# Linear attention, then a top-2 mixture of experts: the order in which the engines' instructions are emitted in the experts with seven products

## The chip, the cores and the metric

One core of one Trainium2 chip runs the kernel. Its time is the device time of one execution in microseconds; what is compared is the median of several runs of each kernel.

## The reference

Shapes: batch 4, 8 heads, 768 positions, 64 channels a head; so 3072 tokens of 512 channels. There are 8 experts with w1 of 512 x 1024 and w2 of 1024 x 512, all in fp32.

```python
# attention with a decay lam[h], in blocks of 64 positions
for b in range(nb):
    intra = einsum('bhic,bhjc->bhij', qb, kb) * Dmask
    intra = einsum('bhij,bhjd->bhid', intra, vb)
    inter = einsum('bhid,bhde->bhie', qb * lam_pow, kv_state)
    out[:, :, sl] = intra + inter
    kv_state = lam_block * kv_state + einsum('bhsd,bhse->bhde', kb * rev_pow, vb)
# mixture: every token goes to its two best experts
noisy = x @ w_gate + log1p(exp(x @ w_noise)) * noise
top2_w = softmax of the two largest of noisy
for e in range(E):
    h = maximum(x[mask] @ w1[e], 0.0)
    out[mask] += top2_w[mask, k, None] * (h @ w2[e])
```

## The kernel before

A first part computes the attention, the gate and the lists of tokens of each expert. Expert 0 and expert 1 then run with plain matrix products. Experts 2 to 7, ordered by how many tokens they have, are what the change is about. Each takes 768 or 800 tokens: six tiles of 128 and, for experts 2 to 4, one tile of 32. Every fp32 operand is split into a high part, which an activation rounds to fp32r, and a low part, the difference, which a subtraction makes; a product is three matmuls (high x high, high x low, low x high).

*First layer.* An expert's 2 x 2 block product (tokens and channels halved) is done with seven block products instead of eight, for each of four pairs of column blocks, f = 0 to 3. Function `first_layer` walks a list of 26 slots, `SEQ`: five for f=0, then seven for each of f = 1, 2, 3, in which products 4 and 3 of f-1 stand between products 2 and 6 of f. Products 4 and 3 of f=3 come later (`ENDS`), after the first 18 matmuls of the second layer. A product is six matmuls (L969) of 384 or 400 columns into a PSUM bank: U, V (four banks named pS) or W (pR or pL). Products 1, 6 and 7 all accumulate in U, and after each ScalarE copies U to SBUF (L992, a tile "ot"); PE's next product into U waits for that copy. The "ot" tiles come from a pool of four buffers, which the stores of turned rows and, in experts 2 to 4, the crossed tiles use as well.

`result` makes the hidden values out of the banks: an add on DVE (L981: bank plus copy), ScalarE's activation for the high part (L975), and the low part, on DVE (L978) or, for products 2 and 7, a further activation (L986) and a subtraction on POOL (L987). All of it stands at the product's own slot. At fixed slots stand besides: the splits of w2 (`split_w`: L829 on ACT, L833 on DVE) and of the column blocks f = 2, 3 of w1 (`split_c`, three groups: L804 on ACT, L805 on DVE; after group 1 four sums of weight blocks on POOL, L808 to L811, which group 2 then splits), the loads of later weights, and for the next expert the gathers of its rows on POOL (L876), each behind a one-element copy "spacer" (L1383), and their turning on DVE (L896) and storing by SP (L898). `gather_prev` (L1038) reads the earlier output.

*Second layer.* `gemm2` multiplies tile by tile into two banks, pO and pKV, by turns; DVE evacuates each (L1080 or L1082) and POOL scatters it to the output (L1126). Experts 2 to 4 do three of the tiles as columns (`columns2`), four steps ahead of the four row tiles. Between tiles `behind` prepares the next expert: `operands` (its split and combined rows: L937 on ACT, L938 and L943 to L946 on DVE) and `split_c` of the blocks f = 0, 1.

The whole program is emitted in a fixed order: every engine does its instructions in the order in which the code emits them. A tile from a pool waits until the instructions that used the buffer before are done.

Of the kernel before, what the change touches and what calls it, by code (L numbers as in the profile page):

```python
# [37 lines left out]
E = 8  # L38
# [85 lines left out]
def kernel(  # L124
# [666 lines left out]
    def split_c(e, f, group):  # L791
# [12 lines left out]
        nc.scalar.activation(hi[:, ks], src, AF.Copy)  # L804
        nc.vector.tensor_tensor(lo[:, ks], src, hi[:, ks].bitcast(FT), op=SUB)  # L805
        if group == 1:
            g = nc.gpsimd
            g.tensor_tensor(a22, a21, a22, op=ADD)  # L808
            g.tensor_tensor(a21, a11, a21, op=SUB)  # L809
            g.tensor_tensor(a11, a22, a11, op=SUB)  # L810
            g.tensor_tensor(a12, a12, a11, op=SUB)  # L811
# [160 lines left out]
    def result(e, f, m, banks):  # L972

        def high(i, k, src):
            nc.scalar.activation(hv(e, 0, i, k), src, AF.Relu)  # L975

        def low(i, k, src, eng):
            eng.scalar_tensor_tensor(hv(e, 1, i, k), src, 0.0, hv(e, 0, i, k).bitcast(FT), op0=OP.max, op1=SUB)  # L978

        def add(i, k, p, x, eng):  # L980
            nc.vector.tensor_tensor(x, p, x, op=ADD)  # L981
            high(i, k, x)
            if eng is nc.vector:
                low(i, k, x, eng)
            else:
                nc.scalar.activation(x, x, AF.Relu)  # L986
                eng.tensor_tensor(hv(e, 1, i, k), x, hv(e, 0, i, k).bitcast(FT), op=SUB)  # L987

        U, V, W = [banks.get(b) for b in "UVW"]
# [12 lines left out]

    LOWS = (nc.gpsimd, nc.gpsimd, nc.vector)
# [359 lines left out]
    def first_layer(e):  # L1363

        banks = {f: {} for f in range(QF)}
        nxt = tile_order(e + 1) if e + 1 < E else []
        for s, (f, m) in enumerate(SEQ):
            product(e, f, m, banks[f])
            result(e, f, m, banks[f])
            pace = banks[f][1][0:1, 0:1]  # L1370
            if s in (0, 2, 12, 17):
                j = (0, 2, 12, 17).index(s)
                split_w(2, e, j)
                if j < 2:
                    load_j(e, j + 2)
            for g, at in enumerate(((5, 12), (8, 15), (9, 16))):
                if s in at:
                    split_c(e, 2 + at.index(s), g)
            if s in (11, 18) and e + 1 < E:
                load_c(e + 1, (11, 18).index(s))  # L1380
            for i, j in enumerate(nxt):
                if s == (0, 1, 4, 7, 9, 14, 16)[i]:
                    nc.gpsimd.tensor_copy(spacer, pace)  # L1383
                    gather_rows(e + 1, j)
                if s == (6, 8, 13, 15, 20, 22, 22)[i]:
                    turn_rows(e + 1, j)
            if s in (2, 5, 10, 12):
                gather_prev(e, (0, 1, 3, 4)[(2, 5, 10, 12).index(s)])
        return banks[QF - 1]

    def behind(e, t, steps):

        if e + 1 == E:
            return
        n = e + 1
# [148 lines left out]
```

## Time and profile before

| | |
|---|---|
| median of 3 runs | 852.26 us (850.43 to 856.97) |
| profiled execution | 848.9 us, its span 847.1 |
| granted clock of TensorE, mean | 0.944 |
| busy: PE, DVE, ACT, POOL | 720.6, 438.8, 337.7, 394.7 us |
| six first layers | 287.8 us |

A busy time is an engine's sum over the span; the matmuls are pipelined, so PE's is no measure of full speed. Where an engine waited, the profile names the instruction whose semaphore came last.

### The profile page before, as it was taken

What the parts mean: (1) busy time and instruction counts of PE and PEld (TensorE: products, weight loads), DVE (VectorE), ACT (ScalarE), POOL (GpSimd) and SP (SyncE); (2) the same over time, 40 slices, a digit from 0 to 9 for tenths busy, and PEclk for the clock granted to TensorE, in tenths of its full rate; (3) what the DMA queues carried; (4) which work ended last, traced back from release to release, by engine and by line L of the source; (5) the groups of instructions that cost most, each with busy time, mean ns of one, the idle gap of its engine ahead of it and who ended that gap; (6) DMA issues with size and microseconds to landing.
All of it is one profiled execution on the core that took longest, in us unless ns stands there. A gap on an engine that the chain in (4) does not pass through costs nothing.

```text
span 847.1 us, 14367 instructions
## 1 busy us (share of the span) xinstructions
PE 720.6 (85%) x4861; PEld 627.0 (74%) x4861; DVE 438.8 (52%) x1009; ACT 337.7 (40%) x670; POOL 394.7 (47%) x569
## 2 busy tenths in 40 slices
PE   6999998999999696887869877987687977798696
PEld 4888887889898585776759666876575766587584
DVE  6348796842655754455454645373435444453421
ACT  2667855112432244423542345324442354235400
POOL 6022657786354557324832385226722573244322
PEclk9999999999999889999999988998998999989998
DMA  9999975652546655337533663347533453343001
GB/s 203 216 252 258 254 210 178 222 121 50 174 126 174 158 136 151 111 85 185 189 110 99 184 175 118 107 127 191 154 108 98 122 183 100 101 119 99 10 37 33
DMA packets 165728, 121.29 MB, mean 143 GB/s; under 512 B 89597, under 2 KB 136829, under 8 KB 165652
## 3 DMA queue, kind: packets, MB, share of 16 engines
q1 hardware_dynamic: 151076, 84.04, 36.7%
q0 software_dynamic: 14160, 35.77, 16.4%
q8 instruction: 39, 0.64, 0.3%
q10 hardware_dynamic: 416, 0.53, 0.2%
q14 instruction: 37, 0.30, 0.1%
HBM read 83.87 MB, written 37.32 MB: 143 GB/s over the span
## 4 chain that ended last, share of the span: by engine, by line
PE 33%; issue 16%; DVE 15%; POOL 14%; ACT 9%; SPq 8%; DMA 5%; POOLq 0%; DVEq 0%; ACTq 0%
PE pS L1016 8%; PE pKV L1064 6%; PE pO L1064 4%; SPq L910 4%; POOL out_dram L1126 3%; ACT ht L975 3%; ACT w L804 3%; DVE ot L981 2%; DVE w L805 2%; PE pS L364 2%; PE pKV L377 2%; SPq L781 2%; PE pS L969 2%; PE pO L377 2%; POOL wst L809 2%
## 5 line engine op out<-in xcount | busy, mean ns | idle before, releaser
L969 PE MATMUL pS<-xa,w 128*128 128x400 f32 (+1 forms) x624 | 183.4, 375 | 82.6 <-ACT ot L992 80.4
L969 PEld LDWEIGHTS pS<-xa,w 128*128 128x128 f32 x624 | 124.2, 205 | 102.5 <-ACT ot L992 96.1
L1064 PE MATMUL pO<-w2h,ht 128*128 128x512 f32 x336 | 113.0, 407 | 13.2 <-DVE pv L1080 6.8
L1064 PE MATMUL pKV<-w2h,ht 128*128 128x512 f32 x336 | 112.9, 407 | 11.5 <-DVE w1b L1080 11.5
L805 DVE TENSOR_TENSOR w<-wst,w 128x512 fp32r<-128x512 f32 (+2 forms) x72 | 56.1, 792 | 116.1 <-ACT w L804 116.1
L987 POOL TENSOR_TENSOR ht<-ot,ht 128x400 fp32r<-128x400 f32 (+1 forms) x48 | 49.3, 1027 | 98.0 <-ACT ot L986 86.6
L804 ACT ACTIVATE w<-wst 128x512 fp32r<-128x512 f32 (+2 forms) x72 | 48.7, 692 | 106.2 <-POOL wst L811 57.9
L969 PE MATMUL pS<-xb,w 128*128 128x400 f32 (+1 forms) x240 | 88.9, 370 | 0.0
L1064 PEld LDWEIGHTS pO<-w2h,ht 128*128 128x128 f32 x336 | 65.9, 196 | 29.4 <-DVE pv L1080 8.1
L1064 PEld LDWEIGHTS pKV<-w2h,ht 128*128 128x128 f32 x336 | 65.8, 196 | 27.3 <-DVE w1b L1080 12.4
L975 ACT ACTIVATE ht<-ot 128x400 fp32r<-128x400 f32 (+1 forms) x72 | 38.2, 531 | 91.3 <-DVE ot L981 91.3
L1016 PE MATMUL pS<-xa,w 128*128 128x256 f32 (+2 forms) x440 | 73.5, 316 | 0.8 <-DVE xa L888 0.4
L1016 PEld LDWEIGHTS pS<-xa,w 128*128 128x128 f32 x440 | 65.3, 189 | 4.8 <-DVE xa L888 0.6
L1064 PE MATMUL pO<-w2l,ht 128*128 128x512 f32 x168 | 68.1, 405 | 0.0
L1064 PE MATMUL pKV<-w2l,ht 128*128 128x512 f32 x168 | 68.0, 405 | 0.0
L833 DVE TENSOR_TENSOR w2l<-wst,w2h 128x1024 fp32r<-128x1024 f32 (+1 forms) x33 | 38.4, 1163 | 44.7 <-ACT w2h L829 44.5
L876 POOL DMA_INDIRECT xr<-x_tok,rec x42 | 48.7, 1161 | 17.1 <-issue 7.5
L631 POOL DMA_INDIRECT lst<-recs,dest x48 | 48.4, 1009 | 11.0 <-issue 8.1
L969 PEld LDWEIGHTS pS<-xb,w 128*128 128x128 f32 x240 | 50.4, 210 | 0.5
L808 POOL TENSOR_TENSOR wst<-wst 128x256 f32<-128x256 f32 x24 | 18.1, 756 | 64.8 <-DVE w L805 55.7
L992 ACT ACTIVATE ot<-pS 128x400 f32<-128x400 f32 (+1 forms) x72 | 34.9, 485 | 30.0 <-PE pS L969 19.3
L937 ACT ACTIVATE xa<-wst 128x512 fp32r<-128x512 f32 (+1 forms) x48 | 24.8, 565 | 53.5 <-DVE wst L946 53.5
(300 smaller groups left out, 1458.7 us busy)
## 6 DMA issues: line engine op xcount, KB each, us to landing
wst<-in_moe_w_dram SPq DMA_DIRECT2D x36, 512.0 KB, 4.5
turned<-ot SPq DMA_DIRECT2D x36, 256.0 KB, 3.5
kt<-in_k_dram SPq DMA_DIRECT2D x24, 256.0 KB, 5.7
qt<-in_q_dram SPq DMA_DIRECT2D x24, 256.0 KB, 6.0
vt<-in_v_dram SPq DMA_DIRECT2D x24, 256.0 KB, 5.7
wst<-in_moe_w_dram SPq DMA_DIRECT2D x48, 128.0 KB, 2.6
wst<-in_moe_w_dram SPq DMA_DIRECT2D x96, 64.0 KB, 2.8
wst<-turned SPq DMA_DIRECT2D x96, 64.0 KB, 2.0
```

Of the source, the lines that this page charges most:

```text
L377: nc.tensor.matmul(PO[u][a][half(g), hp, :], lhs, rhs, start=n == 1, stop=n == (8 if u % NW or a else 4))
L631: st = nc.gpsimd.indirect_dma_start(out=lst, out_offset=bass.IndirectOffsetOnAxis(ap=r["dest"][:, i, c:c + 1], axis=0), in_=r["rec"][:, c, ...
L804: nc.scalar.activation(hi[:, ks], src, AF.Copy)
L805: nc.vector.tensor_tensor(lo[:, ks], src, hi[:, ks].bitcast(FT), op=SUB)
L833: low.tensor_tensor(lo, st, hi.bitcast(FT), op=SUB)
L876: nc.gpsimd.indirect_dma_start(out=xrow(e, t)[:size(e, t)], out_offset=None, in_=x_tok[:rows, :], in_offset=bass.IndirectOffsetOnAxis(ap=a ...
L969: nc.tensor.matmul(p, WO[f % 2][:, a, kw, d, :], xo(x, kx, kx + 1)[:, 0, d, :w], start=first and i == 0, stop=i == 5, skip_group_check=True)
L975: nc.scalar.activation(hv(e, 0, i, k), src, AF.Relu)
L987: eng.tensor_tensor(hv(e, 1, i, k), x, hv(e, 0, i, k).bitcast(FT), op=SUB)
L992: nc.scalar.activation(banks[m], U, AF.Copy)
L1016: nc.tensor.matmul(p, W1[a][d][:, fs], xt(b, cs)[:, d], start=(d == 0 and i == 0), stop=(d == DB - 1 and i == 2))
L1064: nc.tensor.matmul(p, h, W2[b][f // 2][:, f % 2, :], start=(i == 0), stop=(i == len(TERMS) - 1))
```

## The change

`result` no longer emits its instructions but returns lists of them: those for the product's own slot, the next slot and the one after that. Product 7 begins with the next slot and makes its low part on DVE now, from the sum and without the further activation. `first_layer` keeps a table `todo` of what stands at each slot; the lists of `result` are appended to it, after what the table held from the start. The splits, sums, loads, gathers and turnings get slots of their own, the sums of POOL four slots ahead of group 2, the high and low halves of a split mostly a slot apart. The spacer copies in front of the gathers are gone. `behind` is called before a tile instead of after it, and splits groups 0 and 1 (with the sums) a tile ahead of group 2.

```diff
-    def split_c(e, f, group):
+    def split_c(e, f, group, what="hl"):
...
-        nc.scalar.activation(hi[:, ks], src, AF.Copy)
-        nc.vector.tensor_tensor(lo[:, ks], src, hi[:, ks].bitcast(FT), op=SUB)
-        if group == 1:
-            g = nc.gpsimd
-            g.tensor_tensor(a22, a21, a22, op=ADD)
...
+        if "h" in what:
+            nc.scalar.activation(hi[:, ks], src, AF.Copy)
+        if "l" in what:
+            nc.vector.tensor_tensor(lo[:, ks], src, hi[:, ks].bitcast(FT), op=SUB)
+
+    def sums_c(e, f):
...
+        g = nc.gpsimd
+        g.tensor_tensor(a22, a21, a22, op=ADD)
...
     def result(e, f, m, banks):
...
         if m == 2:
-            add(f, 0, W, banks[1], LOWS[0])
-        elif m == 7:
-            add(f + QF, 1, V, banks[7], LOWS[1])
-        elif m == 4:
-            high(f + QF, 0, U)
-            low(f + QF, 0, U, nc.vector)
-        elif m == 3:
-            add(f, 1, V, banks[6], LOWS[2])
-
-    LOWS = (nc.gpsimd, nc.gpsimd, nc.vector)
+            x = banks[1]
+            return [[add(W, x)], [high(f, 0, x), positive(x)], [rest(f, 0, x)]]
+        if m == 7:
+            x = banks[7]
+            return [[], [add(V, x)], [high(f + QF, 1, x)], [low(f + QF, 1, x)]]
+        if m == 4:
+            return [[high(f + QF, 0, U)], [low(f + QF, 0, U)]]
+        if m == 3:
+            x = banks[6]
+            return [[add(V, x)], [high(f, 1, x)], [low(f, 1, x)]]
+        return []
...
     def first_layer(e):
...
+        for j, s in enumerate((1, 6, 13, 20)):
+            at(s, lambda j=j: split_high(2, e, j))
+            at(s + 1, lambda j=j: split_low(2, e, j))
+            if j < 2:
+                at(s + 1, lambda j=j: load_j(e, j + 2))
+        for c, ss in ((2, (3, 8, 12)), (3, (10, 15, 19))):
+            for g, s in enumerate(ss):
+                at(s, lambda c=c, g=g: split_c(e, c, g, "h"))
+                at(s + (g != 1), lambda c=c, g=g: split_c(e, c, g, "l"))
+            at(ss[1], lambda c=c: sums_c(e, c))
+            if e + 1 < E:
+                at(ss[2] + 1, lambda c=c: load_c(e + 1, c - 2))
+        for i, j in enumerate(nxt):
+            at((0, 1, 4, 7, 9, 14, 16)[i], lambda j=j: gather_rows(e + 1, j))
+            at((6, 8, 13, 15, 20, 22, 22)[i], lambda j=j: turn_rows(e + 1, j))
+        for i, j in enumerate((0, 1, 3, 4)):
+            at((2, 5, 10, 12)[i], lambda j=j: gather_prev(e, j))
+
+        def step(s, f, m):
+            product(e, f, m, banks[f])
+            ops = result(e, f, m, banks[f])
+            if ops and s < len(SEQ):
+                for op in ops[0]:
+                    op()
+            for op in todo.pop(s, []):
+                op()
+            if ops and s >= len(SEQ):
+                for op in ops[0]:
+                    op()
+            for i, more in enumerate(ops[1:]):
+                at(s + 1 + i, *more)
...
-            if s in (0, 2, 12, 17):
-                j = (0, 2, 12, 17).index(s)
-                split_w(2, e, j)
-                if j < 2:
-                    load_j(e, j + 2)
-            for g, at in enumerate(((5, 12), (8, 15), (9, 16))):
-                if s in at:
-                    split_c(e, 2 + at.index(s), g)
-            if s in (11, 18) and e + 1 < E:
-                load_c(e + 1, (11, 18).index(s))
-            for i, j in enumerate(nxt):
-                if s == (0, 1, 4, 7, 9, 14, 16)[i]:
-                    nc.gpsimd.tensor_copy(spacer, pace)
-                    gather_rows(e + 1, j)
...
+    def behind(e, t):
...
+        c, x = {1: ((1, 3), (2, 3, 4, 5))}.get(e, ((0, 3), (2, 4, 5, 6)) if e in CROSS else ((0, 2), (1, 3, 4, 5)))
+        for i, k in enumerate(c):
+            if t == k:
+                split_c(n, i, 0)
+                split_c(n, i, 1)
+                sums_c(n, i)
+            if t == k + 1:
+                split_c(n, i, 2)
+                load_c(n, i + 2)
         for p in range(4 if TAILS[n] else 3):
-            if t == at[p]:
+            if t == x[p]:
                 operands(n, p)
...
+            behind(e, t)
+            last(tile)
...
-            behind(e, t, len(steps))
```

## Rows read from the trace of the kernel before

**Rows 1.** Waits of PE, whole span: us in total, times, longest us.

```profile
PE pS L969 <- ACT ot L992: 80.4, 44, 5.1
PE pKV L1064 <- DVE w1b L1080: 11.5, 2, 5.8
PE pO L1064 <- DVE pv L1080: 6.8, 3, 2.4
PE pO L1064 <- DVE w1b L1082: 6.4, 1, 6.4
```

**Rows 2.** Windows: first layers of experts 2 to 7; us and instructions by engine.

```profile
core 0: us, PE busy (x) PEld busy (x) DVE busy (x) ACT busy (x) POOL busy (x), PEclk, DMA share, GB/s
304.84:352.73 47.89, 35.05 (x159) 31.82 (x158) 24.27 (x38) 23.21 (x42) 30.24 (x34) 0.89 0.48 141
393.19:442.85 49.66, 34.62 (x158) 30.83 (x159) 24.14 (x42) 24.30 (x46) 32.24 (x40) 0.93 0.50 144
483.94:533.88 49.94, 35.92 (x159) 32.97 (x158) 23.43 (x37) 24.25 (x45) 32.08 (x38) 0.86 0.49 139
576.48:626.39 49.91, 34.56 (x158) 31.07 (x157) 22.05 (x33) 23.55 (x44) 31.56 (x38) 0.90 0.50 138
670.16:715.66 45.50, 32.62 (x158) 30.09 (x157) 21.89 (x33) 22.09 (x41) 28.18 (x34) 0.92 0.50 141
759.22:804.11 44.89, 33.23 (x158) 29.88 (x157) 18.11 (x27) 21.98 (x41) 19.85 (x22) 0.92 0.23 57
```

**Rows 3.** Timeline of PE in expert 5: start, us, instruction.

```profile
594.38 0.33 PE L969 MATMUL pS<-xb,w 128*128 128x384 f32 x1
...
595.42 0.34 PE L969 MATMUL pS<-xb,w 128*128 128x384 f32 x1
```

**Rows 4.** Windows in expert 5, behind a long wait and later; columns as in rows 2.

```profile
585.20:592.00 6.80, 5.78 (x18) 5.78 (x19) 2.16 (x3) 4.28 (x8) 4.57 (x7) 0.50 0.69 206
597.50:612.00 14.50, 8.42 (x42) 7.15 (x42) 6.27 (x11) 7.01 (x14) 9.86 (x12) 1.00 0.50 150
```

**Rows 5.** Waits of ACT from 300 us on; columns as in rows 1.

```profile
ACT ht L975 <- DVE ot L981: 91.3, 72, 5.0
```

**Rows 6.** Timeline of ACT in expert 5, idle time before in brackets.

```profile
611.55 0.47 ACT L992 ACTIVATE ot<-pS 128x384 f32<-128x384 f32 x1
615.54 1.06 ACT L804 ACTIVATE w<-wst 128x1024 fp32r<-128x1024 f32 x1 [3.52 <-POOL wst L811]
```

**Rows 7.** Timeline of PE at the same place.

```profile
612.08 0.44 PE L969 MATMUL pS<-xa,w 128*128 128x384 f32 x1 [4.69 <-ACT ot L992]
```

**Rows 8.** POOL's instructions by line from 304 us: min/median/max ns, first and last start.

```profile
L987 POOL TENSOR_TENSOR ht<-ot,ht x48: 989/1022/1066, 310.8 to 806.5; 128x400 fp32r<-128x400 f32 x24, 128x384 fp32r<-128x384 f32 x24
L808 POOL TENSOR_TENSOR wst<-wst x22: 720/732/767, 322.4 to 790.1; 128x256 f32<-128x256 f32 x22
L876 POOL DMA_INDIRECT xr<-x_tok,rec x32: 951/1060/2146, 309.0 to 700.0; - x32
```

**Rows 9.** Timeline of POOL: last scatter of the expert before, experts 2 to 6.

```profile
307.14 1.44 POOL L1126 DMA_INDIRECT out_dram<-w1b,rec  x1 [3.13 <-DVE ovi L1334]
...
399.14 1.36 POOL L1126 DMA_INDIRECT out_dram<-ot,rec  x1 [0.27 <-issue]
...
489.15 1.36 POOL L1126 DMA_INDIRECT out_dram<-ot,rec  x1 [0.26 <-issue]
...
582.64 1.35 POOL L1126 DMA_INDIRECT out_dram<-ot,rec  x1 [0.27 <-issue]
...
671.39 1.58 POOL L1126 DMA_INDIRECT out_dram<-ot,rec  x1 [0.51 <-DVE ot L1082]
```

**Rows 10.** Timeline of DVE in the second layer of expert 5.

```profile
638.81 0.68 DVE L938 TENSOR_TENSOR xb<-wst,xa 128x512 fp32r<-128x512 f32 x1
...
642.24 1.29 DVE L938 TENSOR_TENSOR xb<-wst,xa 128x512 fp32r<-128x512 f32 x2 [0.70 <-ACT xa L937]
...
648.80 1.22 DVE L805 TENSOR_TENSOR w<-wst,w 128x1024 fp32r<-128x1024 f32 x1 [4.33 <-ACT w L804]
```

**Rows 11.** DMA issues of the page: KB each, median us from issue to landing.

```profile
turned<-ot SPq DMA_DIRECT2D x36, 256.0 KB, 3.5
```

More of the change, by code (lines that the diff above doesn't have):

```diff
@@ L803, in split_c @@
             ks = slice(0, 2)
[L804 to L811 removed]
+        if "h" in what:
[3 more added lines that the diff above has]
+    def sums_c(e, f):
+        v = WS[1, e, f].rearrange("p (d i c) -> p d i c", d=DB, i=2)
+        a11, a12, a21, a22 = [v[:, 2 * j:2 * j + 2, i, :] for i in range(2) for j in range(2)]
+        g = nc.gpsimd
+        g.tensor_tensor(a22, a21, a22, op=ADD)
+        g.tensor_tensor(a21, a11, a21, op=SUB)
+        g.tensor_tensor(a11, a22, a11, op=SUB)
+        g.tensor_tensor(a12, a12, a11, op=SUB)
     def split_w(which, e, j, half=None, low=nc.vector):
@@ L972, in result, with low, positive, rest @@
     def result(e, f, m, banks):
+        U, V, W = [banks.get(b) for b in "UVW"]
         def high(i, k, src):
[L975 to L989, printed above, removed]
+            return lambda: nc.scalar.activation(hv(e, 0, i, k), src, AF.Relu)
+        def low(i, k, src):
+            return lambda: nc.vector.scalar_tensor_tensor(hv(e, 1, i, k), src, 0.0, hv(e, 0, i, k).bitcast(FT),
+                                                          op0=OP.max, op1=SUB)
+        def positive(x):
+            return lambda: nc.scalar.activation(x, x, AF.Relu)
+        def rest(i, k, x):
+            return lambda: nc.gpsimd.tensor_tensor(hv(e, 1, i, k), x, hv(e, 0, i, k).bitcast(FT), op=SUB)
+        def add(p, x):
+            return lambda: nc.vector.tensor_tensor(x, p, x, op=ADD)
         if m in (1, 6, 7):
@@ L1389, in first_layer, with at @@
-        return banks[QF - 1]
-    def behind(e, t, steps):
-        if e + 1 == E:
-            return
-        n = e + 1
-        at = (1, 4, 5, 6) if e in CROSS else (0, 1, 3, 4) if e > 1 else (1, 2, 4, 5)
+        todo = {}
+        def at(s, *ops):
+            todo.setdefault(s, []).extend(ops)
+        for j, s in enumerate((1, 6, 13, 20)):
[3 more added lines that the diff above has]
+                at(s + 1, lambda j=j: load_j(e, j + 2))
@@ L1401, in behind @@
                     load_j(n, p)
-        for c, k in enumerate((0, 2) if e in CROSS else (0, 2)):
-            if t == k:
-                for g in range(3):
-                    split_c(n, c, g)
-                load_c(n, c + 2)
     def fetch_pairs(e):
@@ L1438 @@
         else:
-            bank = first_layer(e)
+            step, todo = first_layer(e)
         if e == E - 1:
@@ L1452 @@
             next(steps[0])
-            for f, m in ENDS:
-                product(e, f, m, bank)
-                result(e, f, m, bank)
+            for i, (f, m) in enumerate(ENDS):
+                step(len(SEQ) + i, f, m)
+            for s in sorted(todo):
+                for op in todo[s]:
+                    op()
             next(steps[1])
@@ L1462 @@
             prepare(e + 2)
-        for t, step in enumerate(steps):
+        for t, tile in enumerate(steps):
             if e == 1:
                 turn_next(t + FB - LAG)
-            last(step)
+            behind(e, t)
+            last(tile)
             if e in CROSS:
```

11 lines of the change are left out of this document (4 added, 7 removed).

## The prediction

> **What bounds the kernel now.** The waits of PE come first [rows 1]: one kind makes up most of its idle time after the attention, 80.4 us in 44 waits, at most 5.1 us each, of the product line L969 on the ScalarE copy L992. All lie in six stretches, the first layers of experts 2 to 7, which take 47.89, 49.66, 49.94, 49.91, 45.50 and 44.89 us, together 287.8 [rows 2]. The same rows show that no engine is full there: PE is busy 33 to 36 us of each, POOL 20 to 32, DVE 18 to 24, ACT 22 to 24, and the granted clock is 0.86 to 0.93. How little PE needs shows in its timeline: the second matmul of one half product starts at 594.38 and that of the half product after the next at 595.42, so a product at full clock is 1.04 us [rows 3], and by the ratio of the columns 1.08 where it has 400 instead of 384 (experts 2 to 4). Twenty-six products are 27.0 or 28.2 us; three layers of each, 166 us. So 287.8 - 166 = 122 us are idle time or half clock. The clock is the second half of the price of a stall: behind the 5.1 us wait it was granted at 0.50, the 1.2 GHz level, for the whole stretch 585.2 to 592.0, and at 1.00, 2.4 GHz, in 597.5 to 612.0 [rows 4].
>
> Why PE waits is read from ACT: 91.3 us in 72 waits (one for each such activation) of L975 on the add L981 on DVE [rows 5]. ACT takes its instructions in order, so whatever stands behind an add that is not there yet waits too, and L992 is one of them. An example: the copy for slot 16 of expert 5 (product 6 of f=2) is done only at 612.02 [rows 6], and product 7 starts at 612.08 after 4.69 us idle [rows 7]. A second such point is group 2 of a weight split: ACT idles 3.52 us to 615.54 for POOL's last sum, with copies queued behind [rows 6].
>
> **The change, part by part.** (1) *Results over three slots.* The add stays at its slot (for product 7 it moves one slot on), the activation and the subtraction follow one and two slots later. No matmul is added or taken. The copies L992, which PE needs soonest, are still emitted first in their slot, now behind activations whose add was emitted a slot earlier. DVE gets four more subtractions per expert, and POOL loses four of 1.02 us [rows 8]; ACT loses four activations (the positive part for product 7). None of the three was full, so I cost it at nothing: DVE's 18 to 24 us become 20 to 26 beside PE's 27 to 28, and if PE went below that DVE would be the bound. (2) *The spacer copies of POOL go*, and with them the wait of a gather for a copy and of an add for a spacer. The gathers are then paced by POOL's queue alone. (3) *Sums ahead of group 2:* groups 0, 1 and 2 of a column split move from slots 5, 8, 9 and 12, 15, 16 to 3, 8, 12 and 10, 15, 19. The four sums of POOL, 0.73 us each with 0.08 between, 3.3 us in all [rows 8], now have four slots, 4.2 us, before ACT asks for them. The loads of the next two column blocks go from slots 11 and 18 to 13 and 20, those of W2 from 0 and 2 to 2 and 7, and W2's splits from 0, 2, 12, 17 to 1, 6, 13, 20 with the subtraction a slot later. SP issues the loads in order with the stores of the turned rows, and those of slots 13 and 20 now stand right ahead of a store. I cost that below, with the buffers.
>
> What is late next? I follow POOL's queue, since its sums feed group 2, and group 2 feeds products 6, 5, 7 and 3 (slots 16 and 23). POOL is free of the last expert's scatters at 308.58, 400.50, 490.51, 583.99 and 672.97 [rows 9], which is 3.7, 7.3, 6.6, 7.5 and 2.8 us after the starts of experts 2 to 6 [rows 2]. Ahead of the first sums stand four gathers and two reads of earlier output, all indirect transfers, for which I take the gather's 1.06 us [rows 8] and 0.25 of issue as between the scatters [rows 9]: 6 x 1.31 = 7.9; one subtraction 1.0; the sums 3.3. So the sums end 12.2 us after POOL is free. From there: ACT's part of group 2 takes 1.06 us [rows 6] and DVE's 1.22 [rows 10], and slot 16 starts at +2.3. POOL meanwhile does a subtraction, four indirect transfers and the second sums, 1.0 + 5.2 + 3.3 = 9.5, and slot 23 starts 2.3 later, at +11.8, where PE alone would have come at +2.3 + 7 x 1.05 = +9.7. Three products more give +15. One more us I add because the copy of slot 12 may take the buffer that POOL's subtraction of slot 8 gives back: it stands right behind the sums in POOL's queue. So a layer ends 12.2 + 16 = 28.2 us after POOL is free: 31.9, 35.5, 34.8, 35.7 and 31.0 us. Expert 7 has no gathers, so PE sets its time: 27.0 and some 2 of waits, 29.0. Together 197.9 against 287.8: 89.9 us less.
>
> To that I add a reserve of 4.5 us a layer, 27 us. One part is the clock: the 6.8 us at 0.50 in [rows 4] lost half their work, 3.4 us, and I keep half of such a loss, 1.7. The other, 2.8 us, is for waits that such a reckoning leaves out, above all for the four "ot" buffers. A value now holds its buffer two slots longer, and a store of turned rows takes 3.5 us from issue to landing [rows 11]. At the low end this is nothing; at the high end two copies of a layer wait one store each on the path, 7 us, in the five layers with turned rows. I take 2.8, nearer to the low end because two of the four buffers come free by DVE and not by a store. First layers: 89.9 - 27 = 63 us less.
>
> (4) *The second layers* (`behind`). Their waits are evacuations that DVE reaches late: 11.5 us in two for experts 5 and 6, 6.8 in three for experts 2 to 4, 6.4 for expert 1 [rows 1]. In expert 5 DVE idles 4.33 us for group 2, then does 1.22 of it, and only then the evacuation [rows 10]. Now group 2 comes a tile later. For experts 5 and 6 group 2 and the operands still stand ahead of the second tile's evacuation, and the operands alone are 4.7 us of DVE, from 638.81 to 643.53 [rows 10]. The sums start earlier, though, before the first tile's evacuation: the second tile is out some 3 us sooner, and of 5.8 us idle about 3 remain; I take 3 us less each, between 5 less and 1 more. For expert 1 the split group and the operands no longer meet ahead of one evacuation: 5 less, between 8 and 0. For experts 2 to 4 the change puts 4.7 us of operands *ahead* of the first row tile's evacuation, which PE already awaits. That adds up to 4.7 at the place; PE gets some back since fewer operands are left at the end: 2 more each, between 0 and 5. Sum: -5 - 6 + 6 = -5, between -18 and +17.
>
> In all 848.9 - 63 - 5 = 781 us for the profiled execution; it lies 3.4 us under the median of the three runs, 852.26, so on that scale 784.
>
> A rule that speaks against part (1): VectorE now works more beside POOL's sums. In the rows a sum took 0.720 to 0.767 us in all 22 cases, whatever DVE did [rows 8]. The Trainium skill (GPSIMD Engine Reference, 8. Key points) says that GpSimd shares its SBUF interfaces with VectorE, with contention when a DVE instruction has two SBUF inputs. By that the two sums of a layer would lengthen and every layer with them; the trace shows no such spread, so the reckoning stands without it.
>
> **The rivals.** *Buffers bind* (784 + 35 = 819): the high end of the buffer term, two stores of 3.5 us [rows 11] on the path in each of five layers. For it: four buffers, and at slots 20 to 23 all are held, while the stores stand in SP's queue behind six weight loads. Against: the allocator has so far found buffers such that only short waits came of it.
>
> *Nothing but POOL's list binds* (784 - 27 - 8 = 749): the reserve is not needed and the second layers reach the better half of their bounds. For it: after the change no engine waits in order for a chain of its own making. Against: all engines stay coupled.
>
> *The wait stays* (852): ACT's queue is still in order, and group 2 in slots 12 and 19 still stands ahead of copies. If each of the ten indirect transfers ahead of the second sums took twice its 1.31 us, slot 23 would come 13 us later, in five layers 66 us, all of the gain; the change would then do only on paper what it says. Against: POOL idles now; its 32 us of work in a stretch of 50 [rows 2] shrink by over 4.
>
> *Slower, by the clock* (about 874): the few long idle stretches become many short ones, and PE is granted 1.2 GHz nearly throughout. A product then takes 2.08 us, a layer 54 or 56, six of them 331; with a tenth of the work at 2.4 GHz 315, 27 us more than now, of which part (4) gives back 5. It decides from the point where the mean clock of the first layers falls under 166/288 = 0.58. Against it: 597.5 to 612.0 holds several short idle stretches (8.42 us busy of 14.50) at a clock of 1.00 [rows 4]. The Trainium skill (TensorE: Matmul & The Clock Gate, A second HAM failure mode) tells of a kernel whose PE idled briefly between groups of matmuls and whose clock swung between the levels; the stretch named speaks against that here.
>
> **How the numbers follow.** Forecast 784, chance 0.60; buffers bind 0.17; POOL alone 0.13; the wait stays 0.06; slower 0.04. The forecast's own range, with the bounds of part (4), is 771 to 806. To leave out no more than 2 in 10 the whole must reach to 822 for the buffers and into the POOL case, to 755. A measurement tells about 1% from nothing: faster by more than that 0.90, within it 0.06, slower 0.04.
>
> **What would show it.** Right: the six first layers last 30 to 40 us each, the waits of L969 on L992 fall under 30 us, the granted clock there rises to 0.95; L975 no longer waits 91 us for L981; the wait of ACT for POOL's last sum shrinks but does not vanish in experts 3 to 5, being shortest in expert 7. The second layers of experts 2 to 4 get longer, those of 1, 5 and 6 shorter. Wrong, if ACT's copies wait for stores or for POOL in the buffers' name, if POOL's gathers wait for turned rows ahead of the sums, or if DVE, with most of the moved work, becomes the engine that the copies' readers wait for.

## The result, and the profile after

The changed kernel takes 813.3 us (median of 3 runs, 811.66 to 816.01) beside 852.26: ratio 0.9536, 95% interval 0.9463 to 0.961. That is 39 us less, where 68 were forecast; it lies near the rival *Buffers bind* (819). The profiled run has a span of 811.5 us.

In the code after the change the product is L975 (was L969), ScalarE's copy out of bank U L1000 (L992), the activation L983 (L975), the add L996 (L981), GpSimd's subtraction L993 (L987), the weight splits L805 and L807 (L804, L805), the sums L814 to L817 (L808 to L811), the evacuation L1089 (L1080).

Windows of the first layers of experts 2 to 7, columns as in [rows 2]:

```profile
306.70:353.32 46.62, 32.79 (x158) 31.27 (x157) 26.04 (x41) 21.08 (x39) 25.52 (x26) 0.90 0.56 157
397.00:445.78 48.78, 34.78 (x158) 33.35 (x157) 25.80 (x37) 20.36 (x38) 26.71 (x28) 0.83 0.52 153
489.33:533.14 43.81, 34.07 (x159) 32.71 (x158) 24.82 (x36) 20.40 (x38) 25.93 (x27) 0.84 0.50 147
577.35:621.48 44.13, 32.07 (x158) 30.29 (x157) 24.68 (x36) 20.02 (x38) 25.60 (x27) 0.88 0.50 145
659.38:700.63 41.25, 31.12 (x158) 30.17 (x157) 24.06 (x36) 20.02 (x38) 25.20 (x25) 0.92 0.54 148
738.57:768.17 29.60, 28.58 (x158) 27.19 (x157) 21.65 (x30) 20.53 (x38) 19.63 (x19) 1.00 0.35 87
```

Together 254.2 us, 33.6 less than before. Expert 7, which turns no rows for a next expert, came down to 29.6; the other five lost only 1 to 6 us each, and their granted clock is 0.83 to 0.92 still.

The waits of PE that answer to [rows 1], and below them those of ScalarE from 300 us on that answer to [rows 5]:

```profile
PE pS L975 <- ACT ot L1000: 59.6, 19, 5.7
PE pO L1073 <- DVE pv L1089: 13.6, 3, 4.6
PE pKV L1073 <- DVE w1b L1089: 4.9, 4, 1.4
```

```profile
ACT ot L1000 <- POOL ht L993: 45.3, 10, 5.6
...
ACT ot L1000 <- DMA turned<-ot: 23.8, 6, 6.1
...
ACT w L805 <- POOL wst L817: 14.5, 5, 4.1
ACT ot L1000 <- DMA out_dram<-ot,rec: 12.3, 8, 2.4
ACT ot L1000 <- DVE ht L986: 8.6, 6, 1.8
ACT ht L983 <- DVE ot L996: 5.3, 8, 0.8
```

The wait for the add fell from 91.3 us in 72 to 5.3 in 8, as the change means it to. In its place the copies wait before they start, for a buffer to write into: 45.3 us in ten waits, two in each of five layers, for GpSimd's subtraction, and 23.8 for stores of turned rows. PE's waits became fewer (19 for 44) and longer.

One such place, in expert 5: the timelines of ScalarE, of GpSimd and of PE.

```profile
593.08 0.49 ACT L1000 ACTIVATE ot<-pS 128x384 f32<-128x384 f32 x1 [2.51 <-DMA turned<-ot]
...
598.63 0.87 ACT L1000 ACTIVATE ot<-pS 128x384 f32<-128x384 f32 x2 [4.13 <-POOL ht L993]
...
608.91 0.49 ACT L1000 ACTIVATE ot<-pS 128x384 f32<-128x384 f32 x1 [5.44 <-POOL ht L993]
```

```profile
604.79 0.72 POOL L814 TENSOR_TENSOR wst<-wst 128x256 f32<-128x256 f32 x1 [0.48 <-DVE w L807]
605.59 0.72 POOL L815 TENSOR_TENSOR wst<-wst 128x256 f32<-128x256 f32 x1
606.39 0.72 POOL L816 TENSOR_TENSOR wst<-wst 128x256 f32<-128x256 f32 x1
607.20 0.72 POOL L817 TENSOR_TENSOR wst<-wst 128x256 f32<-128x256 f32 x1
607.88 0.99 POOL L993 TENSOR_TENSOR ht<-ot,ht 128x384 fp32r<-128x384 f32 x1
```

```profile
609.45 0.69 PE L975 MATMUL pS<-xa,w 128*128 128x384 f32 x1 [5.67 <-ACT ot L1000]
```

The sums and the subtraction of product 2 belong to one slot, 15 (8 the first time). The table `todo` holds the sums from the start and `result` appends the subtraction, so it comes behind four sums. It is the last reader of the buffer that holds product 1's copy; the copy of slot 16 takes that buffer. The copy runs 0.04 us after the subtraction ends at 608.87, and PE starts 5.67 us late.

The second layers of experts 2 to 4 became longer, 43.68, 43.55 and 44.21 us for 40.46, 41.09 and 42.60 (+7.3); those of experts 5 and 6 shorter, 37.90 and 37.94 for 43.77 and 43.56 (-11.5), as was expert 1's, 39.4 for 45.8 (-6.4). Each is taken from the last matmul of the 26 slots to the first of the next first layer, expert 1's from its first second-layer matmul. One part of the difference isn't the change's: that matmul of expert 1 starts at 267.3 us after and at 259.0 before, with the same work ahead of it. Windows of the changed kernel there:

```profile
139.10:145.90 6.80, 6.54 (x30) 6.14 (x29) 2.42 (x3) 2.06 (x5) 5.33 (x9) 0.50 0.40 130
217.60:221.00 3.40, 3.03 (x9) 2.56 (x10) 1.75 (x3) 2.13 (x4) 2.49 (x4) 0.50 0.75 239
```

In none of the twelve runs below, ten of which have the changed kernel's order up to there, does it start later than 260.9, so kernels are also compared by the time from there to the end: 588.1 before, 544.2 after.

### The profile page after: what moved, and what is told of

It is laid out like the page before. It is cut to its first block, busy times and chain, and to the rows that moved or that the text cites. A ratio compares the mean times of both kernels' runs of the same rounds, so it can differ in the third digit from the quotient of the medians.

```text
span 811.5 us, 14328 instructions
## 1 busy us (share of the span) xinstructions
PE 708.3 (87%) x4861; PEld 626.0 (77%) x4861; DVE 459.9 (57%) x1033; ACT 321.1 (40%) x646; POOL 367.8 (45%) x513
## 4 chain that ended last, share of the span: by engine, by line
PE 34%; DVE 15%; issue 14%; POOL 11%; SPq 10%; DMA 10%; ACT 5%; POOLq 0%; DVEq 0%; ACTq 0%
PE pS L1025 8%; SPq L916 7%; PE pO L1073 4%; PE pS L975 4%; PE pKV L1073 4%; DMA out_dram<-ot,rec 2%; POOL out_dram L1135 2%; PE pKV L377 2%; DVE w2l L839 2%; PE pS L364 2%; DMA xr<-x_tok,rec 2%; PE pO L377 2%; DVE w L807 2%; POOL wst L816 2%; POOL wst L815 2%
## 5 line engine op out<-in xcount | busy, mean ns | idle before, releaser
L975 PE MATMUL pS<-xa,w 128*128 128x400 f32 (+1 forms) x624 | 174.6, 367 | 60.8 <-ACT ot L1000 59.6
L975 PEld LDWEIGHTS pS<-xa,w 128*128 128x128 f32 x624 | 124.3, 204 | 69.5 <-ACT ot L1000 66.6
L1073 PE MATMUL pO<-w2h,ht 128*128 128x512 f32 x336 | 113.1, 407 | 14.8 <-DVE pv L1089 13.6
L1073 PE MATMUL pKV<-w2h,ht 128*128 128x512 f32 x336 | 109.8, 397 | 4.9 <-DVE w1b L1089 4.9
L1000 ACT ACTIVATE ot<-pS 128x400 f32<-128x400 f32 (+1 forms) x72 | 35.3, 497 | 144.9 <-PE pS L975 51.3
L975 PE MATMUL pS<-xb,w 128*128 128x400 f32 (+1 forms) x240 | 88.5, 369 | 0.0
L807 DVE TENSOR_TENSOR w<-wst,w 128x512 fp32r<-128x512 f32 (+2 forms) x72 | 57.7, 815 | 43.5 <-ACT w L805 42.7
L1073 PEld LDWEIGHTS pKV<-w2h,ht 128*128 128x128 f32 x336 | 63.8, 190 | 20.4 <-DVE w1b L1089 6.6
L1025 PE MATMUL pS<-xa,w 128*128 128x256 f32 (+2 forms) x440 | 75.4, 321 | 1.2 <-DVE xa L894 1.2
L805 ACT ACTIVATE w<-wst 128x512 fp32r<-128x512 f32 (+2 forms) x72 | 48.7, 693 | 58.1 <-POOL spacer L1134 43.6
L1073 PE MATMUL pKV<-w2l,ht 128*128 128x512 f32 x168 | 66.3, 395 | 0.0
L814 POOL TENSOR_TENSOR wst<-wst 128x256 f32<-128x256 f32 x24 | 18.4, 769 | 93.2 <-DVE w L807 78.3
L882 POOL DMA_INDIRECT xr<-x_tok,rec x42 | 46.4, 1105 | 19.8 <-issue 7.3
L975 PEld LDWEIGHTS pS<-xb,w 128*128 128x128 f32 x240 | 50.4, 210 | 0.4
L986 DVE SCALAR_TENSOR_TENSOR ht<-ot,ht 128x400 fp32r<-128x400 f32 (+1 forms) x48 | 33.0, 687 | 29.6 <-ACT ht L983 28.6
L996 DVE TENSOR_TENSOR ot<-pS,ot 128x400 f32<-128x400 f32 (+1 forms) x48 | 27.0, 562 | 35.2 <-ACT ot L1000 29.1
L1135 POOL DMA_INDIRECT out_dram<-w1b,rec x15 | 22.0, 1464 | 54.5 <-DVE w1b L1089 32.4
L993 POOL TENSOR_TENSOR ht<-ot,ht 128x400 fp32r<-128x400 f32 (+1 forms) x24 | 25.7, 1073 | 45.6 <-ACT ot L990 45.4
```

Source lines behind the costliest of these rows:

```text
L882: nc.gpsimd.indirect_dma_start(out=xrow(e, t)[:size(e, t)], out_offset=None, in_=x_tok[:rows, :], in_offset=bass.IndirectOffsetOnAxis(ap=a ...
L975: nc.tensor.matmul(p, WO[f % 2][:, a, kw, d, :], xo(x, kx, kx + 1)[:, 0, d, :w], start=first and i == 0, stop=i == 5, skip_group_check=True)
L986: return lambda: nc.vector.scalar_tensor_tensor(hv(e, 1, i, k), src, 0.0, hv(e, 0, i, k).bitcast(FT), op0=OP.max, op1=SUB)
L1025: nc.tensor.matmul(p, W1[a][d][:, fs], xt(b, cs)[:, d], start=(d == 0 and i == 0), stop=(d == DB - 1 and i == 2))
L1073: nc.tensor.matmul(p, h, W2[b][f // 2][:, f % 2, :], start=(i == 0), stop=(i == len(TERMS) - 1))
L1135: st = nc.gpsimd.indirect_dma_start(out=out, out_offset=bass.IndirectOffsetOnAxis(ap=REC[e, t][:, 0:1], axis=0), in_=o, in_offset=None, bo ...
```

## The experiments

The median of before was 845.56, 846.91 and 846.54 us in the three groups of runs, medians of 5 or 6 runs for each kernel. By its ratio the changed kernel would take some 806 to 808 there (800 to 814 by the interval). In the table, "first" is the sum of the six first layers, "second 2-4" that of three second layers, "rest" the time from expert 1's second layer to the end, all by the timeline of PE in each profiled run.

| kernel | us | ratio to before (95%) | first | second 2-4 | rest |
|---|---|---|---|---|---|
| before | | 1 | 287.8 | 124.2 | 588.1 |
| changed | 813.3 | 0.9536 (0.9463 to 0.961) | 254.2 | 131.4 | 544.2 |
| e1_spare | 775.04 | 0.9168 (0.915 to 0.9187) | 223.1 | 133.1 | 514.7 |
| e2_lowdve | 789.94 | 0.932 (0.9293 to 0.9347) | 238.0 | 136.1 | 533.6 |
| e5_restfirst | 787.58 | 0.9309 (0.9291 to 0.9327) | 237.0 | 131.4 | 526.5 |
| e4_before_behind | 835.54 | 0.9865 (0.9844 to 0.9887) | 284.2 | 134.2 | 576.8 |
| e3_before_spare | 852.28 | 1.007 (1.0044 to 1.0095) | 291.9 | 124.1 | 592.0 |
| e6_cross | 792.29 | 0.9362 (0.9342 to 0.9383) | 258.9 | 112.5 | 530.2 |
| e7_wide | 754.14 | 0.8905 (0.8885 to 0.8925) | 200.7 | 133.8 | 493.1 |
| e8_wide_cross | 738.75 | 0.8729 (0.8712 to 0.8746) | 205.0 | 114.4 | 478.2 |
| e11_last_copy | 730.10 | 0.8625 (0.8605 to 0.8645) | 196.4 | 115.5 | 470.6 |
| e10_load_late | 736.87 | 0.8707 (0.8683 to 0.8731) | 192.7 | 125.0 | 476.2 |
| e12_results_now | 798.28 | 0.9422 (0.9398 to 0.9446) | 247.6 | 133.3 | 540.3 |
| e13_sums_late | 795.86 | 0.9394 (0.9367 to 0.942) | 242.0 | 135.6 | 535.8 |

**Do the buffers bind?** Three ways to free them sooner. e1_spare puts product 1's copies into a tile that lies unused then (`WX[0]`), and two reads of earlier output move to later slots for it:

```diff
-            banks[m] = hp.tile([128, DM], FT, name="ot", bufs=4)[:, :columns_of_half(e)]
+            x = hp.tile([128, DM], FT, name="ot", bufs=4) if m > 1 else WX[0][:, f % 2 * DM:(f % 2 + 1) * DM]
+            banks[m] = x[:, :columns_of_half(e)]
-            at((2, 5, 10, 12)[i], lambda j=j: gather_prev(e, j))
+            at((2, 5, 16, 23)[i], lambda j=j: gather_prev(e, j))
```

> The changed kernel, except that the copies of product 1 no longer take one of the four rotating buffers: they go into the two 512-column halves of a tile that lies unused until the old output rows of tiles 3 and 4 are fetched into it; those two fetches move from slots 10 and 12 to slots 16 and 23. Theory A (the buffers hold the first layers back: a copy waits until GpSimd's subtraction or a turned row's store has freed one): ScalarE's waits of 45.3 us for GpSimd in front of copies vanish, the first layers of experts 2 to 6 lose some 4 us each, the total falls by 20 (12 to 28) to about 793 us. Rival B (GpSimd's list and the parts' conversions bind anyway, the buffers only take the blame): the waits move to the conversion behind the sums or to TensorE's wait for weights, first layers stay within 1 us each, total 808 to 818 us.

e2_lowdve makes product 2's low part on DVE:

```diff
-            return [[add(W, x)], [high(f, 0, x), positive(x)], [rest(f, 0, x)]]
+            return [[add(W, x)], [high(f, 0, x)], [low(f, 0, x)]]
```

> The changed kernel with the low part of product 2 computed by VectorE, as for product 3, in place of ScalarE's rectification and GpSimd's subtraction; four GpSimd and four ScalarE instructions fewer in each first layer, four more of VectorE. Theory A (the buffers bind, through GpSimd's subtraction standing behind the sums): copies no longer wait for GpSimd, first layers of experts 2 to 6 lose about 3 to 4 us each, total about 797 us (788 to 804). Rival B (not the buffers: any of the three engines' lists is as full): what GpSimd gives back VectorE takes, total 808 to 820 us.

e5_restfirst puts the subtraction of slots 8 and 15 ahead of the sums:

```diff
-            at(ss[1], lambda c=c: sums_c(e, c))
...
             for op in todo.pop(s, []):
                 op()
+            if s in (8, 15):
+                sums_c(e, 2 + (s > 8))
```

> The changed kernel with one tie turned round: in slots 8 and 15 GpSimd gets the subtraction of product 2's low part ahead of the four sums, not behind them. Theory A: the copies in slots 11 and 16 find their buffer some 3 to 4 us earlier, the sums end about 1 us later; the first layers of experts 2 to 6 lose 3 us each, total about 798 us (790 to 806). Rival B: the later sums push the conversion of their results and with it the products of the next quarter by as much as is won, total 808 to 820 us.

All three came out as theory A: 775.04, 789.94 and 787.58 us, e1 and e5 below the range given, e2 within it. That is some 31, 16 and 19 below the changed kernel by the ratios, and 29.5, 10.6 and 17.7 by "rest" (e2's profiled run was its longest). GpSimd's list wasn't shortened in e5, only two entries were exchanged. What ScalarE's copies still wait for in e1 and in e5:

```profile
ACT ot L1001 <- DVE ht L986: 33.1, 20, 3.7
...
ACT ot L1001 <- DMA turned<-ot: 12.9, 2, 6.9
ACT w1b L1001 <- DMA out_dram<-w1b,rec: 5.2, 1, 5.2
```

```profile
ACT ot L1000 <- DVE ht L986: 26.6, 16, 2.9
...
ACT ot L1000 <- POOL ht L993: 21.6, 5, 4.9
```

In e1 no copy waits for GpSimd's subtraction any more. What is left stands in the name of buffers again: the copies of products 6 and 7, whose last reader is DVE, and stores.

**Did they bind before?** e3_before_spare is the edit of e1 in the old kernel.

> Control: the kernel before with the same relief as in the run that took product 1's copies out of the four rotating buffers (they go to the unused tile, the two fetches move to slots 16 and 23). Theory A in its sharp form (the buffers bind only once the results no longer stand in the lists): in the old order every product is held by the addition and by the sums before a buffer is ever missed, so no change, 842 to 850 us against about 846. Rival B (the relief helps any order, and the 31 us that it gave the changed kernel say nothing about the change): 815 to 830 us.

It is 0.7% slower than before, not faster. The same relief is worth some 30 us in the new order and nothing in the old: it is the change that made the buffers bind.

**The rest of the relief.** e7_wide takes product 7's copies out too:

```diff
-            banks[m] = hp.tile([128, DM], FT, name="ot", bufs=4)[:, :columns_of_half(e)]
+            i = (f + (e == 2)) % 2
+            x = {1: WX[0][:, i * DM:(i + 1) * DM], 7: (PV[0], zero)[f % 2]}.get(m)
+            banks[m] = (hp.tile([128, DM], FT, name="ot", bufs=4) if m == 6 else x)[:, :columns_of_half(e)]
-            at((2, 5, 10, 12)[i], lambda j=j: gather_prev(e, j))
+            at((22, 29, 23 if e == 2 else 16, 16 if e == 2 else 23)[i], lambda j=j: gather_prev(e, j))
```

> The changed kernel with the copies of products 1 and 7 out of the rotating buffers: product 1's into the two halves of the unused tile, product 7's into the two tiles of old output rows of tiles 0 and 1; the four fetches of old rows move to slots 22, 29, 16 and 23 (16 and 23 exchanged in expert 2, whose spare halves come free in the other order). Theory A: what is left of ScalarE's buffer waits in the first relief (33 us for VectorE's low parts, 13 us for turned rows' stores, 5 us for a scatter) goes for the most part; first layers of experts 2 to 6 fall to 32 to 38 us each, the total to about 757 us (748 to 766). Rival B (the remaining waits are as long as the conversions behind them): 768 to 778 us, as with product 1 alone. Rival C (late fetches hold the evacuation of the first tile): second layers of experts 5 and 6 longer by 3 us or more.

It took 754.14 us, as theory A had it; the second layers of experts 5 and 6 stayed at 37.9, which speaks against rival C. But the edit does two things: all four reads of earlier output now stand behind GpSimd's second sums. By the timelines of GpSimd those sums end 27.5, 30.6, 30.1, 30.6 and 28.2 us after the start of a layer (experts 2 to 6) in the changed kernel and 24.7, 26.6, 26.0, 25.6 and 26.1 in e7, together 18 us sooner. From there to the end of the layer it is 19.1, 18.2, 13.7, 13.5 and 13.0 us and 13.5, 12.8, 5.7, 5.6 and 5.6, together 34 us less. So of the 53.5 us that the first layers lose, 34 lie behind the sums, where the copies wait; the 18 ahead may be the moved reads as well as the buffers, and no run separates the two. e5 moves no read; its first layers lose 17.2.

**The second layers alone.** e4_before_behind is the old kernel with the new `behind`, called ahead of the tile; the sums stay in the conversion.

> The kernel before with the second layers' part of the change alone: the conversions for the next expert are issued ahead of a tile and not behind it, in the slots of the changed kernel; first layers keep the old order and the sums stay inside the conversion. By the terms measured in the changed kernel: expert 1 -6.4, experts 2 to 4 +7.3, experts 5 and 6 -11.5, in all -10.6 us, so about 841 us (836 to 848), first layers at their old 48 to 58 us. If instead the second layers' gain came only from the first layers' new order, the total stays at 850 to 854 us.

10.0 us less than before, where 10.6 was worked out from the changed kernel. By the timeline it is 6.5 less for expert 1, 10.0 more for experts 2 to 4 and 11.4 less for experts 5 and 6, and 3.6 less in the first layers. So this part stands by itself. e6_cross then moves one thing in the changed kernel, three of the four operands of experts 2 to 4 (`CROSS`) one step later:

```diff
-        c, x = {1: ((1, 3), (2, 3, 4, 5))}.get(e, ((0, 3), (2, 4, 5, 6)) if e in CROSS else ((0, 2), (1, 3, 4, 5)))
+        c, x = {1: ((1, 3), (2, 3, 4, 5))}.get(e, ((0, 3), (2, 5, 6, 7)) if e in CROSS else ((0, 2), (1, 3, 4, 5)))
```

> The changed kernel with one edit in the second layers of experts 2 to 4: the operands of the next expert stand ahead of steps 2, 5, 6 and 7 and not 2, 4, 5 and 6, which is where the kernel before had them. Theory A (operands ahead of the tile put its evacuation late, TensorE waits 4.4 to 4.6 us for VectorE's evacuation in each of the three): the three second layers lose 3 to 4 us each unless the operands then end late for the next first layer; total 796 to 801 us against about 806 on this chip. Rival (the wait for the evacuation is there in the old order too and only changes place): within 3 us of 806.

792.29 us, some 15 less, a little past the range of theory A. Windows of the second layers of experts 2 to 4 in e6:

```profile
343.71:381.13 37.42, 37.42 (x206) 32.86 (x204) 22.78 (x51) 12.62 (x25) 8.91 (x14) 0.99 0.45 136
431.71:469.76 38.05, 37.88 (x205) 33.21 (x203) 22.77 (x51) 12.60 (x25) 9.19 (x14) 0.98 0.46 136
515.59:552.65 37.06, 37.06 (x204) 32.74 (x204) 22.77 (x51) 12.42 (x23) 8.85 (x14) 1.00 0.56 162
```

PE is busy nearly throughout; the changed kernel's three waits for the evacuation, 13.6 us, are gone, and the first layers give back only 4.7.

**Both together, and the last store.** e8_wide_cross joins e7 and e6:

> Both of the last two edits together: products 1 and 7 out of the rotating buffers and the operands of experts 2 to 4 one step later. If the two are independent, the time is that of the wide relief less what the later operands give alone: 745 to 755 us by theory A for both; if the operands are then late for the next first layer, no less than the wide relief alone.

738.75 us: both gains add up. Its longest wait left, in expert 2, in the timelines of ScalarE, PE and SP's queue:

```profile
332.00 0.50 ACT L1002 ACTIVATE ot<-pS 128x400 f32<-128x400 f32 x1 [6.12 <-DMA turned<-ot]
```

```profile
332.56 0.70 PE L975 MATMUL pS<-xa,w 128*128 128x400 f32 x1 [5.98 <-ACT ot L1002]
```

```profile
324.47 4.58 SPq L781 DMA_DIRECT2D wst<-in_moe_w_dram  x6
329.16 1.53 SPq L904 DMA_DIRECT2D turned<-ot  x3
```

The copy waits for a store that SP issues only behind six weight loads, those of slot 20. The next two edits are shown against the kernel that they build on. e11_last_copy gives that copy another tile (product 6, f=3, experts 2 to 4, into `PV[0]`, whose fetch moves to slot 30), e10_load_late besides puts the six loads behind the fetches of turned rows:

```diff
-            banks[m] = (hp.tile([128, DM], FT, name="ot", bufs=4) if m == 6 else x)[:, :columns_of_half(e)]
+            banks[m] = (x if m != 6 else PV[0] if f == QF - 1 and e in CROSS else hp.tile([128, DM], FT, name="ot", bufs=4))[:, :columns_of_half(e)]
```

> The wide relief with the later operands, and one more copy taken out of the rotating buffers: in experts 2 to 4 the last copy of product 6 (slot 23) goes into the tile of old output rows of tile 0, whose fetch moves to slot 30. In the run without it this copy waited 6.1 us for a turned row's store in experts 2 and 3, and TensorE 6.0 us behind it. Theory A (that store is the last place where buffers bind): first layers of experts 2 and 3 lose 6 us each, total 727 us (724 to 731). Rival B (the turned rows themselves are late: their fetches end at 340 us whatever TensorE does, and the next operands wait for them): the time comes back in the second layers, total 735 to 740 us.

```diff
-            if e + 1 < E:
+            if e + 1 < E and (c == 2 or e not in CROSS):
                 at(ss[2] + 1, lambda c=c: load_c(e + 1, c - 2))
...
+            if e in CROSS:
+                load_c(e + 1, 1)
```

> The last kernel with one more edit for experts 2 to 4: the load of the second quarter of the next expert's weights, eight-odd DMA issues on SyncE at 4.6 us, stands behind the fetches of turned rows and not ahead of the last turned stores. If the fetches bind the next operands (rival B of the last kernel): 3 to 5 us less in each of three experts, total 8 to 14 us below that kernel. If they don't: no change within 2 us, or up to 3 us an expert more where the weights then come late.

e11: 730.10 us, within the range of theory A: its first layers of experts 2 and 3 are 5.2 us shorter each than e8's, expert 4's is 2.1 longer, and the second layers give back 1.1. e10 is 6.8 us slower than e11, the second case of its expectation: its first layers are shorter by 3.7 together, but the second layers of experts 2 and 3 take 42.4 and 44.4 us for 38.6 and 38.6. The weights now come late, ScalarE waits for them there (7.7 us in two) and evacuations stand behind. e11 is the best version of the study, 13.75% below before (interval 13.55 to 13.95). Its first layers:

```profile
300.23:332.62 32.39, 29.61 (x159) 28.18 (x158) 26.18 (x40) 21.57 (x39) 23.73 (x24) 1.00 0.59 170
371.23:406.90 35.67, 30.83 (x158) 27.92 (x159) 26.71 (x44) 22.45 (x43) 27.48 (x30) 1.00 0.61 171
445.53:480.39 34.86, 30.68 (x158) 28.02 (x159) 26.66 (x44) 22.47 (x43) 27.27 (x29) 1.00 0.63 174
518.61:552.24 33.63, 29.52 (x158) 27.02 (x157) 23.22 (x34) 22.08 (x41) 26.94 (x28) 1.00 0.62 169
590.16:621.52 31.36, 29.20 (x158) 27.03 (x157) 23.13 (x34) 20.42 (x38) 23.19 (x22) 1.00 0.57 161
659.45:687.94 28.49, 28.15 (x158) 27.24 (x157) 20.61 (x30) 20.42 (x38) 16.19 (x17) 1.00 0.29 65
```

**What did the list and the lead of the sums bring?** The list is what spreads a result over three slots. e12_results_now takes it away and puts the whole result at the product's own slot; e13_sums_late takes most of the sums' lead:

```diff
-                for op in ops[0]:
+                for op in sum(ops, []):
                     op()
...
-            for i, more in enumerate(ops[1:]):
-                at(s + 1 + i, *more)
```

> The changed kernel without the list for results: addition, rectification and low part of a product all stand in the product's own slot as before; the sums stay four to five slots ahead of their conversion, and the second layers are the changed ones. It tells how much of the first layers' gain is the list's. By the prediction ScalarE's wait for the addition (91.3 us in 72 before) comes back: first layers of 44 to 52 us, total 825 to 838 us against about 807 for the changed kernel. If the place of the sums carries the gain: 805 to 815 us.

```diff
-            at(ss[1], lambda c=c: sums_c(e, c))
+            at(ss[2] - 1, lambda c=c: sums_c(e, c))
```

> The changed kernel with the sums in slots 11 and 18, one ahead of the conversion of their results, and not 8 and 15; the list for results stays. By the prediction the lead of the sums is worth the wait of 3 to 4 us twice a layer: total 820 to 840 us. By what the run with the subtraction ahead of the sums showed, later sums also free GpSimd for the subtractions of slots 8 and 15 and so the buffers; if that weighs as much, 798 to 815 us.

Both came out below every range given for them. e12, without the list, took 798.28 us: its "rest" is 3.9 us shorter than the changed kernel's. The wait for the add is back in full, and yet its first layers are 40.2 us shorter than before's:

```profile
ACT ht L983 <- DVE ot L996: 87.4, 69, 3.5
...
ACT w L805 <- POOL wst L817: 12.1, 3, 4.0
```

What went away in e12 is the other wait that the prediction named, ScalarE's for GpSimd's last sum. Before it was, from 300 us on,

```profile
ACT w L804 <- POOL wst L811: 57.9, 15, 6.0
```

of which 39.9 us in twelve, two a layer, stood in the six first layers. In e12 none stands there. The size is that of the 40.2 us; that the one is the cause of the other is an inference from the sizes.

In e12 the subtraction of product 2 stands in slots 6 and 13, ahead of the sums, so the tie isn't there. The list is therefore weighed against e5, where it isn't there either: ratio 0.9309 with the list, 0.9422 without, some 10 us. Of the 10.6 us between their first layers 9.1 lie in expert 7 (31.1 for 40.2) and 1.5 in the other five. With the list the copies of those five still wait for buffers, as e5's rows above show; no run takes the list away where the buffers are free, so what it is worth there stays open. e13 took 795.86 us. Against e5, which differs in the slot of the sums alone, the lead is worth some 7 us, 5.0 of it in the first layers; ScalarE's wait for the last sum comes back there only to 11.0 us in nine. Against the changed kernel the late sums are a gain, since they let the subtraction pass.

## Why the prediction was right in its direction, and where its sum failed

*The reserve for the buffers was the term that was mis-sized.* The prediction took 2.8 us a layer for waits on the four "ot" buffers and 1.7 for the clock behind them, 27 in all, "because two of the four buffers come free by DVE and not by a store". The prediction's own sum has 6.5 us from the end of GpSimd's second sums to the end of a layer; the changed kernel took 77.5 in five layers, 45 more than that, waits on buffers and slow clock together. So the term was short by some 18 of the 29 us that are missing in the first layers (63 forecast, 33.6 measured). The argument left out the third way in which a buffer comes free. The prediction did say that a copy may take the buffer that GpSimd's subtraction gives back, right behind the sums, and put 1 us on it; it stood there twice a layer, with waits of up to 5.6 us, and exchanging two entries (e5) gave some 18 us back.

*GpSimd's own queue was reckoned too short.* From its last scatter to the end of the second sums the changed kernel took 23.8, 24.8, 24.3, 24.8 and 24.8 us where 21.7 was reckoned, 14 us in all; it was free 3 us sooner than before, taken together, which leaves the other 11 us of the 29. One part is a wait that the sum of the instructions leaves out, of a read of earlier output for a scatter to land, here in expert 5:

```profile
587.79 1.00 POOL L1047 DMA_INDIRECT pv<-out_dram,rec  x1 [1.93 <-DMA out_dram<-ot,rec]
```

*The reckoning without the reserve came out in sum, in part by luck.* It gave 31.9, 35.5, 34.8, 35.7, 31.0 and 29.0 us for the six first layers, 197.9 together. In e11 they are 32.4, 35.7, 34.9, 33.6, 31.4 and 28.5, together 196.4. Behind the second sums e11 took 7.5, 7.5, 7.5, 5.5 and 5.6 us, about the 6.5 reckoned. But up to there it took 21.2, 20.9, 20.1, 19.7 and 22.4 us for the 21.7 reckoned with the four reads of earlier output still ahead, which by the prediction's price are 5.2 us a layer. So the model without waits on buffers is near, and two errors in it, the reads gone and the queue slower than its sum, cancel. The changed kernel wasn't such a kernel yet; in expert 7, which has no turned rows, it nearly was: 29.6.

*Why PE waits was read wrongly in part.* The prediction took ScalarE's 91.3 us of waits for the add [rows 5] as the cause. e12 has 87.4 us of them and first layers 40.2 us shorter than before. So most of that wait was not what set the time of experts 2 to 6 here; in expert 7, where no rows are turned, the list that removes it is worth 9.1 us. The wait for the last sum, which the prediction named second, fits the 40 us in size. Of the edits to the first layers that e12 keeps (the places of splits, sums and loads, the spacer copies gone, product 7's low part on DVE), none was tried alone but the slot of the sums; how the 40 us divide among the others stays open.

*Costed at nothing:* four more DVE subtractions a layer. DVE is busy 22 to 26 us of each layer after, as the 20 to 26 given, and e2, which puts four more on it, is faster still. Right.

*The second layers* came to -10.6 where -5 was forecast, inside -18 to +17. Expert 1 -6.4 (-5 forecast) and experts 2 to 4 +7.3 (+6) were right in size and place: the changed kernel waits 4.6, 4.6 and 4.4 us for an evacuation behind the operands. Experts 5 and 6 lost 5.9 and 5.6 us each where 3 were taken; the wait of 5.8 went to two of together 2.4. e6 shows that the +7.3 was no price of the rest: one step later the three layers take 112.5 us, 11.7 less than before.

*The signs given:* the wait on the copies was to fall under 30 us and stood at 59.6, the clock to rise to 0.95 and stood at 0.83 to 0.92 in five layers and 1.00 in expert 7; the first layers were all outside 30 to 40, five above it and expert 7's just below. ScalarE's wait for the last sum was to stay in experts 3 to 5 and be shortest in expert 7; in the first layers it stands in expert 7 alone, 2.4 us. The wait for the add went as said, and the second layers got longer and shorter where they were to. The sign for "wrong", copies that wait for stores or for GpSimd in the buffers' name, is what the trace shows. Of the rivals *Buffers bind* (819) was the nearest in time and right in kind. Its 819 counts 2.8 us a layer twice, since the forecast that it adds 35 to holds them already; five layers of 4.2 more make 805, so that the measured time lies between the two. It priced two stores in each of five layers; stores made 23.8 us of ScalarE's waits and the subtraction 45.3. *Slower, by the clock* was to decide under a mean clock of 0.58; the lowest layer was granted 0.83.

*Unexplained* is the later start of expert 1's second layer in the run after, 8.2 us; the windows above show two stretches there at a granted clock of 0.50, but not why. Before that matmul ScalarE idles once 8.6 and once 6.9 us with no instruction of the core named as what ended it; the traces of before and e12 have no such wait. The later start makes the measured gain look smaller: by "rest" alone it is 43.9 us.

## What to carry to other kernels

When instructions are moved to a later slot, list for every buffer its last reader in the new order, the engine that this reader stands on and what stands ahead of it there; with few buffers this sets the time more than the engines' busy sums do. Look at ties: two entries of one slot on one in-order engine, where the first is long and the second frees a buffer, cost some 18 us here, and exchanging them is free. A large sum of waits on an in-order engine is no gain to be had until something shows that the work behind it could go earlier.

## What the runs showed of the hardware

GpSimd's sums and DVE's instructions slow each other where they overlap, which the rows before hid because DVE did little beside them: next to 78 of the 88 sums from 300 us on it did nothing. In the changed kernel, expert 5, timelines of GpSimd and DVE:

```profile
594.73 0.94 POOL L815 TENSOR_TENSOR wst<-wst 128x256 f32<-128x256 f32 x1
595.75 1.06 POOL L816 TENSOR_TENSOR wst<-wst 128x256 f32<-128x256 f32 x1
```

```profile
591.61 0.55 DVE L986 SCALAR_TENSOR_TENSOR ht<-ot,ht 128x384 fp32r<-128x384 f32 x1
...
594.02 1.06 DVE L986 SCALAR_TENSOR_TENSOR ht<-ot,ht 128x384 fp32r<-128x384 f32 x1
```

A sum of 0.72 us (at 605.59, above) takes 0.94 and 1.06 here, and DVE's subtraction with both inputs in SBUF 1.06 where it takes 0.55 at 591.61. The 41 sums of this trace with DVE idle beside them took 0.72 to 0.75. The prediction had set this aside on the rows of before, which could not speak on it. The Trainium skill (GPSIMD Engine Reference, 8. Key points) names such contention for DVE instructions with two SBUF inputs, and this trace agrees. It is some 0.6 us in the first sums of this layer, too little to move the forecast.

The clock: in the changed kernel five layers with single idle stretches of up to 5.7 us were granted 0.83 to 0.92. In e11, with 2.2 to 4.8 us idle in the same layers, no stretch of it over 1.6 us, it was 1.00 in all six.
